# Three kernels in one: the first weight piece's low part moved to GpSimd, the second chunk's gates moved ahead, fewer filler products, later casts

## The chip, the cores and the metric

The kernel runs on one core of a Trainium2 chip. The metric is the device time of one execution in microseconds, the median of several runs. A core has five engines with a queue each: TensorE (matrix products and transposes, PE in the profile), VectorE (DVE), ScalarE (ACT), GpSimd (POOL) and SyncE (SP, which here issues nearly all loads). They run side by side and wait for each other through semaphores; inside one queue the order is that of the program.

## The reference

An mLSTM layer over 2 batches, 8 heads, 768 steps and 40 features, then two mixtures of 8 experts over the 1536 tokens (320 wide, 1024 hidden). The first mixture runs every expert on every token and weighs them by a normalised matrix; the second sends each token to one expert.

```python
# mLSTM, per step t
m_new = np.maximum(f_gate[:, :, t] + m, i_gate[:, :, t])
f_stab = np.exp(f_gate[:, :, t] + m - m_new)
i_stab = np.exp(i_gate[:, :, t] - m_new)
C = f_stab * C + i_stab * einsum('bhd,bhe->bhde', vt, kt)
n = f_stab * n + i_stab * kt
y = sigmoid(o_gate) * (C @ qt) / np.maximum(np.abs(n . qt), 1.0)
...
# first mixture
logits = x @ w_gate
...
for e in range(E):
    out += P[:, e:e + 1] * (np.maximum(x @ w1[e], 0.0) @ w2[e])
# second mixture: the same product, only for the expert with the largest logit
```

## The kernel before

The sequence is cut into 12 tiles of 128 tokens (6 chunks of each batch, the batches alternating). `attn(i)` is a generator for tile `i`: each `yield` is a step, and the program decides by hand when to take the next one. In order, its steps are: the transposes of queries and keys (`turn`), the matrix of decay weights `W` (a product of `R` and the gates, then Relu, Exp, and on GpSimd a masking, `affine_select`, L250, a small copy `wl`, L255, and the scaled keys `ku`, L256), the score products (L268), the next tile's loads, the score product on VectorE (L274), the numerator products on TensorE (L282, in two halves), the numerators and denominators on VectorE (L292 to L308), the state product (L314), the transposes of the result (`transpose_x`, which writes `xh`, the rounded copy, and `xl`, the remainder), and the new state `cbd`. Tiles 0 and 1 are `lead` tiles: they run before anything else, interleaved by hand with `steps(...)`.

`gates(c)` prepares chunk `c` of the gates in eight steps on VectorE, two of which have work on GpSimd too: a scan, two differences, a second scan (L160), a rounding copy (L162) and remainders. `make_R(i)` builds the matrix for tile `i` on VectorE.

The first mixture computes each product of float32 numbers as several products of a rounded part and a remainder. A weight piece comes in by `load_chunk`; `split_chunk` casts it on ScalarE into its high part (L482) and subtracts on VectorE for its low part (L488), then issues the next load. The first expert has three pieces of `w1` (0 to 2) and three of `w2`. `s1_unit` computes one feature tile of 128 of the hidden layer: eight products over three blocks of the inner dimension, then Relu on ScalarE (`hh`, L730) and the remainder on VectorE (`hl`, L731). The first item has two tiles of tokens (0 and 1) and eight feature tiles. In the middle of each feature tile (`mid`) and behind it the program calls a background step `bg_early(u)`, with `u` counting them; the tables `RT`, `AT`, `GT`, `DT` and `OT` say at which `u` a matrix, an attention tile, a chunk of gates, its decays or an output gate's sigmoid starts, and each active generator takes one step per call.

`keep_warm(n, cols)` issues products of a constant whose result nobody reads. The order of the whole start is written out by hand:

```python
        steps(f0, g1, g1)
        steps(f1)
        emit_const1()
        steps(f0, f0)
        keep_warm(4, 256)
        steps(f1, f1)
        low = split_chunk(wait=True)
```

Of the kernel before, what the change touches and what calls it, by code (L numbers as in the profile page):

```python
# [12 lines left out]
ALU = mybir.AluOpType  # L13
# [5 lines left out]
def mlstm_moe_moe_kernel(ctx, tc, q, k, v, i_gate, f_gate, o_gate, wg1, w1a, w2a, wg2, w1b, w2b, out):  # L19
    nc = tc.nc  # L20
    pe, act, dve, pool, sp = nc.tensor, nc.scalar, nc.vector, nc.gpsimd, nc.sync
# [179 lines left out]
    def make_R(i):  # L201
# [12 lines left out]
                              in1=mask[:, b * H + hs.start:b * H + hs.stop].unsqueeze(2).to_broadcast([128, H // n, L]), op=ALU.mult)  # L214
        Rs[i] = R

    def attn(i, ps=pst, lead=False):

        b, c = TILES[i]
# [19 lines left out]
        for g in range(2):  # L239
            pw = ps()  # L240
            pe.matmul(pw, gl_[:, c * L:(c + 1) * L], R[:, 4 * g:4 * g + 4, :].rearrange("k h t -> k (h t)"), start=True, stop=True)
            Wg = W[:, 4 * g:4 * g + 4, :].rearrange("s h t -> s (h t)")
            if i == 0 and g == 0:
                keep_warm(1, 256)
            if lead and g == 1:
                dve.tensor_scalar(out=Wg, in0=pw, scalar1=-1.0, scalar2=0.0, op0=ALU.mult, op1=ALU.max)
            else:
                act.activation(out=Wg, in_=pw, func=AF.Relu, scale=-1.0)
            act.activation(out=Wg, in_=Wg, func=AF.Exp, scale=-1.0)
            pool.affine_select(out=W[:, 4 * g:4 * g + 4, :], in_=W[:, 4 * g:4 * g + 4, :], pattern=[[0, 4], [1, L]],  # L250
                               compare_op=ALU.is_ge, fill=0.0, base=0, channel_multiplier=-1)
        if c < NCH - 1:
            u = ku[i % 2]
            wl = atp.tile([128, H, 1], F32, tag="wl", name="wl")
            pool.tensor_copy(wl, W[:, :, L - 1:L])  # L255
            pool.tensor_tensor(out=u[:, :, 0:D], in0=ks[j][:, :, 0:D], in1=wl.to_broadcast([128, H, D]), op=ALU.mult)  # L256
        yield
        if not lead:
            turn(qs[j], qT)
# [6 lines left out]
        for p in range(4):  # L266
            for a in range(2):
                pe.matmul(sc[a][:, p * L:(p + 1) * L], kT[64 * a:64 * a + D, p, :], qT[64 * a:64 * a + D, p, :], start=True, stop=True)  # L268
        yield
        load_tile(i + NB, "qk")  # L270
        yield
        for a in range(2):
# [440 lines left out]
    def s1_unit(t0, nt, ft, mid, cold=False):  # L713
        n = nt * L
        cols = slice(t0 % 4 * L, t0 % 4 * L + n)
        xh_, xl_ = xh[t0 // 4], xl[t0 // 4]
        fs = slice(ft * 128, (ft + 1) * 128)
        p = ps1()[:, 0:n]
        pe.matmul(p, w1h[:, 0, fs], xh_[:, 0, cols], start=True, stop=False)  # L719
        pe.matmul(p, w1h[:, 0, fs], xl_[:, 0, cols], start=False, stop=False)  # L720
        pe.matmul(p, w1l[:, 0, fs], xh_[:, 0, cols], start=False, stop=False)  # L721
        pe.matmul(p, w1h[:, 1, fs], xh_[:, 1, cols], start=False, stop=False)  # L722
        mid()
        pe.matmul(p, w1h[:, 1, fs], xl_[:, 1, cols], start=False, stop=False)  # L724
        pe.matmul(p, w1l[:, 1, fs], xh_[:, 1, cols], start=False, stop=False)
        if cold:
            keep_warm(3, 256)
        pe.matmul(p, w1h[:, 2, fs], xh_[:, 2, cols], start=False, stop=False)
        pe.matmul(p, w1l[:, 2, fs], xh_[:, 2, cols], start=False, stop=True)  # L729
        act.activation(out=hh[:, ft, 0:n], in_=p, func=AF.Relu)  # L730
        dve.scalar_tensor_tensor(out=hl[:, ft, 0:n], in0=p, scalar=0.0, in1=f32(hh[:, ft, 0:n]), op0=ALU.max, op1=ALU.subtract)  # L731
# [18 lines left out]
    def moe1(bg):  # L750
# [44 lines left out]
        for n, (t0, nt, e) in enumerate(ITEMS):  # L795
            newe = n > 0 and (ITEMS[n - 1][2] != e)
            nxt = n + 1 < len(ITEMS) and ITEMS[n + 1][2] != e
            sv, nsv = seven(n), seven(n + 1)
            s2 = pieces(n)
            total = len(s2)  # L800
            sums = make_sums() if nxt and nsv else None
            if sv:
                wide = t0[1] is not None
                todo = left_over
                left_over = []
                nf = 2 if wide else 3

                def step(j, k):
                    if newe and ((j, k) in ((0, 0), (0, 1), (1, 2)) if wide else j < 3 and k == 2):
                        split_chunk(hi=None if wide else pool)  # L810
                    if sums is not None and (wide or j < 3 and k == 2):
                        for _ in range(2 if wide else 3):
                            next(sums, None)
                s1_seven(t0, lambda x: todo[x](), lambda x: s2[x]() if x < nf else None, step)
                s2 = s2[nf:]
                first = nf
            else:
                assert not left_over
                for ft in range(NF):
                    s1_unit(t0, nt, ft, lambda: bg(n, 2 * ft), n == 0 and ft == 0)  # L820
                    if newe and (ft < 3 if n < EARLY - 2 else ft in (0, 2, 4)) or n == 0 and ft in (2, 4, 6):
                        split_chunk()
                    if sums is not None and ft > 3:
                        next(sums, None)
                        next(sums, None)
                    bg(n, 2 * ft + 1)
                first = 0
            if n == CLASSIC - 1:
                close_x()
                open_late()  # L830
            work = make_w() if nxt and nsv else None
            x2 = make_x(1) if n == SEVEN else None
            for x, f in enumerate(s2):
                u = first + x
                if nsv and u >= total - 2:
                    left_over.append(f)
                else:
                    f()
                if n == SEVEN:
                    for _ in range(2):  # L840
                        next(x2, None)
                if work is not None:
                    next(work, None)
                elif nxt and not nsv and u in ((3, 5, 7) if sv else (1, 3, 5)):
                    split_chunk()
                if not sv:
                    bg(n, 2 * NF + u)
            if work is not None:
                drain(work)
# [584 lines left out]
    with tc.manual_schedule():  # L1434
# [27 lines left out]
        def steps(*fs):  # L1462
            for f in fs:
                next(f)
# [4 lines left out]
        steps(f0, f1)  # L1469
        steps(f0, g1, g1)  # L1470
        steps(f1)
        emit_const1()
        steps(f0, f0)
        keep_warm(4, 256)
        steps(f1, f1)
        low = split_chunk(wait=True)
        for t in range(2):
            act.activation(out=so[t], in_=so[t], func=AF.Sigmoid)
        act.preload_act_table(AF.Exp)
        keep_warm(3)  # L1480
        steps(f0, f0, f0)
        steps(f1)
        steps(f0)
        low()
        keep_warm(2)
        steps(f1, f1, f1)
        steps(f0)
        steps(f1)
# [7 lines left out]
        load_tile(3, "o")  # L1496
        active = [g1, g1]

        RT = {3: 2, 6: 3, 17: 4, 27: 5, 37: 6, 47: 7, 55: 8, 63: 9, 71: 10, 79: 11}
        AT = {5: 2, 8: 3, 20: 4, 30: 5, 40: 6, 50: 7, 58: 8, 66: 9, 74: 10, 82: 11}  # L1500
        GT = {6: 2, 26: 3, 43: 4, 59: 5}
        DT = {5: 1, 20: 2, 36: 3, 54: 4, 70: 5}
# [142 lines left out]
```

## Time and profile before

| | |
|---|---|
| median of 3 runs | 948.32 us (948.24 to 949.23) |
| the profiled execution | 948.92 us |
| its span, first to last instruction | 947.1 us |
| mean granted TensorE clock | 0.997 of full speed |
| TensorE busy | 924.8 us, 98% of the span |
| VectorE, ScalarE, GpSimd busy | 625.7, 457.9, 249.3 us |

The times of the rows are microseconds from the start of the span. Busy time of TensorE is modelled at the end of each product, so a busy TensorE is not one at its peak; the spans of GpSimd's instructions are rough. The chain of waits follows the work that ended last back through what released each step: what stands on it sets the end, what does not is hidden.

### The profile page before, as it was taken

Reading aid. Unit: us, or ns where it says so; the run is one execution under the profiler, and the core shown is the slowest. Engines: PE = TensorE matmul, PEld = TensorE weight load, DVE = VectorE, ACT = ScalarE, POOL = GpSimd, SP = SyncE. Lnnn points to the kernel's source line nnn. Section 1 sums busy time; section 2 is a strip of 40 time slices with the busy share of each in tenths; the row PEclk is TensorE's granted clock in tenths of the full one; section 3 lists DMA queues with packets and bytes.
Section 4 is the critical chain, followed back from the end, with each engine's and each line's share of the span. In section 5 each row is a group of like instructions: output and inputs, shape, how many; then the busy total and the mean of one; then the engine's idle time right before and its main releaser. Section 6 shows DMA issues by size and latency. Waiting matters only on the chain.

```text
span 947.1 us, 15365 instructions
## 1 busy us (share of the span) xinstructions
PE 924.8 (98%) x5729; PEld 832.3 (88%) x5729; DVE 625.7 (66%) x1324; ACT 457.9 (48%) x802; POOL 249.3 (26%) x267
## 2 busy tenths in 40 slices
PE   8999999999999999999999999999999999899995
PEld 6888888988999998999998889999889988678995
DVE  8767766667766877475755748485535468965772
ACT  5666546343445565252535535253432144565662
POOL 4323321001006341406041141502231012324411
PEclk9999999999999999999999999999999999999998
DMA  9825431333334103021210302122090034687540
GB/s 198 193 42 113 101 85 34 90 87 102 88 93 133 58 1 117 17 78 56 78 57 3 115 17 81 53 78 66 22 368 30 15 99 117 211 244 224 154 116 20
DMA packets 93711, 91.28 MB, mean 96 GB/s; under 512 B 54845, under 2 KB 82495, under 8 KB 93632
## 3 DMA queue, kind: packets, MB, share of 16 engines
q1 hardware_dynamic: 91424, 83.50, 31.5%
q0 software_dynamic: 2208, 6.75, 2.2%
q8 instruction: 47, 0.77, 0.3%
q14 instruction: 32, 0.26, 0.1%
HBM read 86.29 MB, written 4.76 MB: 96 GB/s over the span
## 4 chain that ended last, share of the span: by engine, by line
PE 89%; DVE 5%; ACT 2%; issue 2%; DMA 1%; POOL 1%; SPq 0%; DVEq 0%; POOLq 0%; ACTq 0%
PE a L619 17%; PE s L735 8%; PE s L736 8%; PE s L737 8%; PE s L1293 4%; PE a L735 3%; PE a L737 3%; PE a L736 3%; PE s L619 3%; PE a L282 2%; PE s L719 2%; PE s L724 2%; PE s L1226 2%; PE s L729 2%; PE s L721 2%; PE s L722 2%
## 5 line engine op out<-in xcount | busy, mean ns | idle before, releaser
L735 PE MATMUL s<-w2h,hh 128*128 128x320 f32 x544 | 171.4, 315 | 0.0
L737 PE MATMUL s<-w2h,hl 128*128 128x320 f32 x544 | 168.2, 309 | 0.0
L736 PE MATMUL s<-w2l,hh 128*128 128x320 f32 x544 | 168.1, 309 | 0.0
L488 POOL TENSOR_TENSOR w2l<-raw,w2h 128x960 fp32r<-128x960 f32 (+1 forms) x24 | 50.0, 2096 | 228.8 <-ACT w2h L482 228.5
L735 PEld LDWEIGHTS s<-w2h,hh 128*128 128x128 f32 x544 | 102.3, 188 | 2.0
L736 PEld LDWEIGHTS s<-w2l,hh 128*128 128x128 f32 x544 | 102.4, 188 | 1.6
L737 PEld LDWEIGHTS s<-w2h,hl 128*128 128x128 f32 x544 | 102.1, 188 | 0.1
L730 ACT ACTIVATE hh<-s 128x512 fp32r<-128x512 f32 (+1 forms) x88 | 49.1, 558 | 95.9 <-PE s L729 95.8
L731 DVE SCALAR_TENSOR_TENSOR hl<-s,hh 128x512 fp32r<-128x512 f32 (+1 forms) x88 | 56.3, 640 | 57.5 <-ACT hh L730 56.0
L619 PE MATMUL a<-th,w 128*128 128x512 f32 (+1 forms) x224 | 80.5, 366 | 0.0
L619 PE MATMUL a<-ts,wx 96*128 96x512 f32 (+1 forms) x192 | 70.7, 368 | 0.5 <-DVE wx L601 0.5
L735 PE MATMUL a<-w2h,hh 128*128 128x320 f32 x224 | 69.3, 309 | 0.0
L737 PE MATMUL a<-w2h,hl 128*128 128x320 f32 x224 | 69.2, 309 | 0.0
L736 PE MATMUL a<-w2l,hh 128*128 128x320 f32 x224 | 69.1, 309 | 0.0
L763 DVE SCALAR_TENSOR_TENSOR acc<-s,probs,acc 128x320 f32<-128x320 f32 x68 | 37.3, 548 | 39.3 <-PE s L737 38.9
L654 ACT COPY pu<-a 128x512 f32<-128x512 f32 (+1 forms) x32 | 17.1, 533 | 88.3 <-PE a L619 82.9
L646 DVE SCALAR_TENSOR_TENSOR hl<-s,hh 128x512 fp32r<-128x512 f32 (+1 forms) x64 | 39.6, 619 | 30.0 <-ACT hh L642 30.0
L642 ACT ACTIVATE hh<-a 128x512 fp32r<-128x512 f32 (+1 forms) x64 | 34.9, 546 | 36.9 <-DVE a L649 34.4
L646 DVE SCALAR_TENSOR_TENSOR hl<-a,hh 128x512 fp32r<-128x512 f32 (+1 forms) x64 | 39.9, 623 | 15.1 <-ACT hh L642 12.4
L619 PEld LDWEIGHTS a<-th,w 128*128 128x128 f32 x224 | 42.3, 189 | 5.8
L619 PE MATMUL a<-tl,w 128*128 128x512 f32 (+1 forms) x128 | 46.9, 366 | 0.0
L736 PEld LDWEIGHTS a<-w2l,hh 128*128 128x128 f32 x224 | 42.1, 188 | 1.5
(389 smaller groups left out, 2430.0 us busy)
## 6 DMA issues: line engine op xcount, KB each, us to landing
raw<-in_moe_w_dram SPq DMA_DIRECT2D x30, 512.0 KB
raw<-in_moe_w_dram SPq DMA_DIRECT2D x30, 480.0 KB
raw<-in_moe_w_dram SPq DMA_DIRECT2D x39, 320.0 KB
raw<-in_moe_w_dram SPq DMA_DIRECT2D x40, 256.0 KB
wr<-in_moe_w_dram SPq DMA_DIRECT2D x8, 1024.0 KB
w2raw<-in_moe_w_dram SPq DMA_DIRECT2D x12, 640.0 KB
raw<-in_moe_w_dram SPq DMA_DIRECT2D x42, 128.0 KB
q<-in_q_dram SPq DMA_DIRECT2D x12, 160.0 KB
```

The lines of the kernel that those rows point to most:

```text
L282: pe.matmul(pn[:, h * V:(h + 1) * V], W[:, h, :], vs[j][:, h, :], start=True, stop=True)
L488: eng.tensor_tensor(out=l, in0=rv, in1=f32(h), op=ALU.subtract)
L619: pe.matmul(bank, w, x, start=(first and n == 0), stop=(n == 3), skip_group_check=True)
L642: act.activation(out=hh[:, f, c], in_=p, func=AF.Relu)
L646: dve.scalar_tensor_tensor(out=hl[:, f, c], in0=p, scalar=0.0, in1=f32(hh[:, f, c]), op0=ALU.max, op1=ALU.subtract)
L730: act.activation(out=hh[:, ft, 0:n], in_=p, func=AF.Relu)
L731: dve.scalar_tensor_tensor(out=hl[:, ft, 0:n], in0=p, scalar=0.0, in1=f32(hh[:, ft, 0:n]), op0=ALU.max, op1=ALU.subtract)
L735: pe.matmul(p[:, 0:DM], hh[:, f, c], w2h[:, w[n], :], start=(first and n == 0), stop=False)
L736: pe.matmul(p[:, 0:DM], hh[:, f, c], w2l[:, w[n], :], start=False, stop=False)
L737: pe.matmul(p[:, 0:DM], hl[:, f, c], w2h[:, w[n], :], start=False, stop=(last and n == len(cuts) - 1))
L763: dve.scalar_tensor_tensor(out=acc[:, tt, 0:DM], in0=p[:, 0:DM], scalar=probs[:, tt, e:e + 1], in1=acc[:, tt, 0:DM], op0=ALU.mult, op1=ALU ...
L1293: pe.matmul(p, a[:, k, fs], b[:, k, xs], start=(k == 0 and n == 0), stop=(k == 2 and n == 1))
```

## The change

Five edits, all in the first 45 us of the program:

- The low part of the first weight piece is taken by GpSimd instead of VectorE. It is issued inside tile 1's attention, ahead of tile 1's scaled keys, which wait behind it on GpSimd.
- Four of the gate steps of chunk 1 are taken between tile 1's score products and its score product on VectorE; before, the background did them during the first feature tiles. The constants of `emit_const1` follow. The matrix of tile 2 is built at background step 2 instead of 3.
- The fillers in the start are fewer: `keep_warm(3)` becomes `keep_warm(2, 256)` and `keep_warm(2)` becomes `keep_warm(1, 256)`.
- In the first feature tile the products that need only the rounded tokens come first, those with the remainders later.
- The three pieces of the first `w2` are split behind feature tiles 2, 5 and 7 instead of 2, 4 and 6.

```diff
@@ attn(i)
+        def make_ku():
+            pool.tensor_tensor(out=ku[i % 2][:, :, 0:D], in0=ks[j][:, :, 0:D], in1=wl.to_broadcast([128, H, D]), op=ALU.mult)
         if c < NCH - 1:
-            u = ku[i % 2]
             wl = atp.tile([128, H, 1], F32, tag="wl", name="wl")
             pool.tensor_copy(wl, W[:, :, L - 1:L])
-            pool.tensor_tensor(out=u[:, :, 0:D], in0=ks[j][:, :, 0:D], in1=wl.to_broadcast([128, H, D]), op=ALU.mult)
+            if i != 1:
+                make_ku()
...
         yield
+        if i == 1:
+            low0[0]()
+            make_ku()
         load_tile(i + NB, "qk")
@@ s1_unit
-        pe.matmul(p, w1h[:, 0, fs], xh_[:, 0, cols], start=True, stop=False)
-        pe.matmul(p, w1h[:, 0, fs], xl_[:, 0, cols], start=False, stop=False)
-        pe.matmul(p, w1l[:, 0, fs], xh_[:, 0, cols], start=False, stop=False)
-        pe.matmul(p, w1h[:, 1, fs], xh_[:, 1, cols], start=False, stop=False)
-        mid()
-        pe.matmul(p, w1h[:, 1, fs], xl_[:, 1, cols], start=False, stop=False)
-        pe.matmul(p, w1l[:, 1, fs], xh_[:, 1, cols], start=False, stop=False)
+        six = [(w1h, xh_, 0), (w1h, xl_, 0), (w1l, xh_, 0), (w1h, xh_, 1), (w1h, xl_, 1), (w1l, xh_, 1)]
+        if cold:
+            six = [six[z] for z in (0, 2, 3, 5, 1, 4)]
+        for z, (w, x, k) in enumerate(six):
+            if z == 4:
+                mid()
+            pe.matmul(p, w[:, k, fs], x[:, k, cols], start=(z == 0), stop=False)
@@ moe1
-                    if newe and (ft < 3 if n < EARLY - 2 else ft in (0, 2, 4)) or n == 0 and ft in (2, 4, 6):
+                    if newe and (ft < 3 if n < EARLY - 2 else ft in (0, 2, 4)) or n == 0 and ft in (2, 5, 7):
                         split_chunk()
@@ the start
         steps(f1)
-        emit_const1()
         steps(f0, f0)
         keep_warm(4, 256)
-        steps(f1, f1)
-        low = split_chunk(wait=True)
+        steps(f1)
+        low0.append(split_chunk(pool, wait=True))
+        steps(f1, g1, g1, g1, g1)
+        emit_const1()
         for t in range(2):
             act.activation(out=so[t], in_=so[t], func=AF.Sigmoid)
         act.preload_act_table(AF.Exp)
-        keep_warm(3)
+        keep_warm(2, 256)
         steps(f0, f0, f0)
         steps(f1)
         steps(f0)
-        low()
-        keep_warm(2)
+        keep_warm(1, 256)
         steps(f1, f1, f1)
...
-        RT = {3: 2, 6: 3, 17: 4, 27: 5, 37: 6, 47: 7, 55: 8, 63: 9, 71: 10, 79: 11}
+        RT = {2: 2, 6: 3, 17: 4, 27: 5, 37: 6, 47: 7, 55: 8, 63: 9, 71: 10, 79: 11}
```

## Rows read from the trace of the kernel before

**Rows 1.** The page, part 1: busy time, share of the span, instructions.
```profile
PE 924.8 (98%) x5729; PEld 832.3 (88%) x5729; DVE 625.7 (66%) x1324; ACT 457.9 (48%) x802; POOL 249.3 (26%) x267
```
**Rows 2.** Windows: stretch, length, busy by engine, granted clock, DMA share, GB/s.
```profile
20.00:24.00 4.00, 3.05 (x19) 2.11 (x20) 3.86 (x8) 0.98 (x3) 0.00 (x0) 1.00 1.13 254
...
30.00:40.00 10.00, 8.95 (x80) 7.76 (x80) 6.33 (x14) 9.31 (x20) 5.76 (x11) 1.00 0.82 167
40.00:50.00 10.00, 10.00 (x84) 10.00 (x84) 7.88 (x19) 2.34 (x5) 0.92 (x2) 1.00 0.65 131
```
**Rows 3.** Chain of waits, 17 to 40 us: start, length, engine, tile, line.
```profile
17.19 1.14 DVE w L488
...
22.42 1.24 DVE w L488
...
25.06 0.39 ACT hh L730
...
33.95 0.88 ACT w2h L482
...
35.05 0.67 PE a L227 x4
...
39.15 0.82 PE a L282 x8
```
**Rows 4.** Timeline of VectorE, 14 to 25 us: start, length, line, operation, [idle before].
```profile
14.06 1.29 DVE L274 TENSOR_TENSOR W<-s,W 128x512 f32<-128x512 f32 x2 [1.00 <-POOL wl L255]
15.58 0.17 DVE L292 COPY num<-a 128x8 f32<-128x8 f32 x1 [0.22 <-PE a L282]
...
16.06 0.17 DVE L301 SCALAR_TENSOR_TENSOR den<-num 128x8 f32<-128x8 f32 x1
...
17.11 1.22 DVE L488 TENSOR_TENSOR w<-raw,w 128x1024 fp32r<-128x1024 f32 x1
...
23.56 0.27 DVE L158 TENSOR_TENSOR acc<-acc 16x128 f32<-16x128 f32 x1
23.87 0.41 DVE L160 TENSOR_TENSOR_SCAN acc<-msk,acc 16x128 f32<-16x128 f32 x1
...
24.88 0.20 DVE L162 CAST gx<-acc 16x128 fp32r<-16x128 f32 x1
```
**Rows 5.** Timeline of GpSimd, 12 to 15 us.
```profile
12.56 1.21 POOL L250 TENSOR_SCALAR_AFFINE_SELECT W<-W 128x512 f32<-128x512 f32 x2
13.84 0.19 POOL L255 COPY wl<-W 128x8 f32<-128x8 f32 x1
14.12 0.72 POOL L256 TENSOR_TENSOR ku<-k,wl 128x320 f32<-128x320 f32 x1
```
**Rows 6.** Line 488 on GpSimd, 675 to 690 us: ns min/median/max, first and last start.
```profile
L488 POOL TENSOR_TENSOR w<-raw,w x3: 2413/2415/2421, 681.0 to 685.8; 128x1024 fp32r<-128x1024 f32 x3
```
**Rows 7.** Timelines of VectorE and GpSimd, 68 to 71 and 862 to 866 us.
```profile
69.78 0.84 DVE L160 TENSOR_TENSOR_SCAN acc<-msk,acc 16x128 f32<-16x128 f32 x1
...
68.54 1.81 POOL L250 TENSOR_SCALAR_AFFINE_SELECT W<-W 128x512 f32<-128x512 f32 x2 [3.29 <-ACT W L249]
...
864.38 1.17 DVE L1250 TENSOR_TENSOR oid<-acc,big 128x1 int32<-128x1 f32 x1
...
862.47 3.06 POOL L1199 TENSOR_TENSOR w2l<-w2raw,w2h 128x640 fp32r<-128x640 f32 x2
```
**Rows 8.** Timelines of VectorE, ScalarE and GpSimd, 27 to 38 us.
```profile
27.86 1.16 DVE L488 TENSOR_TENSOR w2l<-raw,w2h 128x960 fp32r<-128x960 f32 x1 [0.15 <-ACT w2h L482]
...
34.87 1.59 DVE L488 TENSOR_TENSOR w2l<-raw,w2h 128x960 fp32r<-128x960 f32 x1 [0.46 <-DMA wgr<-in_moe_w_gate_dram]
...
37.34 1.27 DVE L274 TENSOR_TENSOR W<-a,W 128x512 f32<-128x512 f32 x2
...
36.22 0.39 ACT L730 ACTIVATE hh<-s 128x256 fp32r<-128x256 f32 x1
...
34.72 0.72 POOL L256 TENSOR_TENSOR ku<-k,wl 128x320 f32<-128x320 f32 x1
```

More of the change, by code (lines that the diff above doesn't have):

```diff
@@ L215, in make_R @@
         Rs[i] = R
+    low0 = []
     def attn(i, ps=pst, lead=False):
```

## The prediction

> **What bounds the kernel now.** I read the page first. TensorE is busy 98% of the span [rows 1], so a change elsewhere can pay only where TensorE waits. Next the stretches of the start: 20 to 24 us holds 3.05 us of TensorE work in 4.00, 30 to 40 us holds 8.95 in 10, from 40 us on there is no gap, and the granted clock is 1.00 in all of them [rows 2]. So the change acts on about 0.95 + 1 us of idle time, plus products that merely fill waits. Third, the chain of waits says whose work fills the gaps [rows 3]. From 15.58 to 23.66 us it is almost wholly VectorE's: the numerators of tile 0, the low part of the first weight piece (17.19), those of tile 1, the second low part, four small splits, the third low part (22.42). TensorE's last product of the first feature tile waits for that third one. From 25.06 to 35.05 us the chain is ScalarE's; the last part of it is the cast of the second output-weight piece (33.95, 0.88 us). With the key transposes at 35.05 it passes to TensorE. Two things can therefore move the end: the time at which VectorE finishes the third low part, and the time at which ScalarE lets those transposes go.
>
> **The low part on GpSimd.** VectorE spends 1.22 us on it, 1.14 of them on the chain [rows 3, 4]. The same shape costs GpSimd 2.41 us [rows 6]. It follows the small copy at 13.84 and would run from about 14.1 to 16.5. VectorE now ends it at 18.33 (17.19 + 1.14) and nobody waits for it then, so it is hidden; a delay beyond 18.3 would use up what cover there is. Before it leaves GpSimd, four things queue: the scaled key tile of tile 1 (0.72 us, [rows 5]), two gate steps, and the memsets of the constants. The scaled key tile then ends near 17.6 us; TensorE reads it behind the transposes of tile 0, which wait for tile 0's numerators (17.19 now), so it is hardly late. The load issued behind the low part goes into SP's queue three issues earlier, ahead of tile 4's queries and keys, which nothing reads before tiles 2 and 3 are through: nothing. VectorE's 0.22 us wait before the numerators (15.35 to 15.58, for TensorE) goes as well, since two filler products of 256 columns replace three of 512. Gross gain: 1.14 + 0.22 = 1.36 us.
>
> **The gates in the idle stretch.** VectorE stands still for 1.00 us before the score product at 14.06 [rows 4]. Three gate steps go there; undisturbed they need 0.31 + 0.44 + 0.24 = 0.99 us (starts at 23.56 and 23.87, then 0.41 and 0.20 with the usual step). They would just fit and cost nothing. But GpSimd is masking tile 1's weights at that time, 12.56 to 13.77 [rows 5], and the two engines do disturb each other. The same scan, started at 69.78 during two such maskings, took 0.84 us against 0.41, and the maskings 1.81 against 1.21 [rows 4, 5, 7]. At 864.38 a one-element instruction of VectorE took 1.17 us: it ended when the second of GpSimd's two subtractions did (862.47 + 3.06 = 865.53) [rows 7]. An instruction with both inputs in SBUF waits out GpSimd's whole instruction. The score product, with one input from PSUM, does not: 1.29 us for two, with GpSimd's multiplication beside it [rows 4, 5]. So I price the three steps at the idle 1.00 us plus 0.4 us, the scan's measured excess; bounds 0 and a whole GpSimd instruction (a rival below).
>
> The Trainium skill says this as a rule ("SBUF — State Buffer", section "Who interferes with whom"): VectorE's second SBUF input comes through a read port shared with GpSimd, the one that issues second blocks until the other has finished, and issue order alone decides. The trace agrees with it at 864.38. Taken at its word it gives either nothing or a full 2.4 us for each meeting, instead of the 0.4 and 0.5 us that I use.
>
> **The same conflict in the numerators.** With the score product 0.4 us late (14.45 to 15.74), the numerators of tile 0 start at 15.74. Two instructions read PSUM; the denominator, 0.48 us later as now (15.58 to 16.06 [rows 4]), so near 16.25, has both inputs in SBUF and meets the low part, which then runs from about 14.45 to 16.85. Price 0.5 us (bounds 0 and 0.6). The normalising product meets the scaled key tile: 0.2 us (0 and 0.5, from the 0.72 us of [rows 5]). Tile 1's chain meets the two gate steps: 0.1 us (0 to 0.3).
>
> Sum for VectorE's chain: 1.36 − 0.4 − 0.5 − 0.2 − 0.1 = **0.16 us** earlier, between −0.4 and +1.36.
>
> **Edits priced at nothing.** The new order of the first tile's products lets four of them run before tile 1's low parts are there, but the last still waits for the third low part (22.42 + 1.24), so the end of that tile does not move. If that cover went (the third low part ready before the products), the order would be worth part of the 0.95 us that TensorE is idle in that stretch [rows 2]. The three gate steps that leave the stretch after 23.56 and the weight matrix of tile 2 built one step earlier free VectorE and TensorE inside a stretch that ScalarE sets from 25.06 to 35.05 [rows 3]: nothing. Tile 2's matrix now stands ahead of the second feature tile's low part on VectorE and delays it; the bank that this low part frees is wanted only behind tile 2's matrix products on TensorE, and these wait for the same matrix. If ScalarE were not the bound there, these edits would be worth up to the 0.92 us that the three instructions' steps take. Of the fillers taken away only those ahead of tile 0's numerator products stood before waiting work, and they are counted above (the 0.22 us); the others shorten TensorE's queue where it waits for VectorE anyway.
>
> **The casts one feature tile later.** Now the second cast sits between the fifth feature tile's activation and the small decay activations that free the bank for tile 3's key transposes. Without it these start 0.88 us sooner, at 34.17 instead of 35.05, and everything behind them on TensorE follows: tile 2's numerator products, now at 39.15, could start at 38.27. But they need the score product, and VectorE's queue now has the second low part ahead of it. That one waits for the cast, which follows the sixth activation (ends 36.61 now [rows 8], 35.73 then): cast to 36.61, low part 1.16 us (27.86; the 1.59 at 34.87 met GpSimd's multiplication at 34.72, which will be over), first half of the score product 0.64 (half of 1.27) gives 38.45 with the steps between. So VectorE, not TensorE, is last there, and the gain is 39.15 − 38.45 = 0.7 us; less 0.1 for the new wait's own signal I take **0.6 us**. Bounds: 0.1, if the low part is again stretched by 0.43 to 0.44, and 0.88. The third cast falls behind the eighth activation; its piece is wanted by the last part of the output stage, well behind the numerator products at 39.15.
>
> **The sum.** 0.16 + 0.6 = 0.76 us. The profiled execution took 948.92 us (span 947.1, and 1.8 us around it), so it would become 948.16. It lies 0.60 above the median of the runs, 948.32, and taken from that the forecast is **947.6 us**, 0.08% less. Behind 40 us TensorE has no gap for 10 us [rows 2], so what it gains there should last.
>
> **Rivals.** *VectorE keeps the whole gain* (chance 0.19): the meetings happen in other gaps and cost nothing. For it: the starts differ by a few tenths, GpSimd's spans are rough, and each price above supposes that two instructions meet. Against it: three meetings would all have to miss. Then 1.36 + 0.6 to 0.88, about 946.3. *The gates lose the port* (0.12): the place is 14.2 us. The scan or the cast after it must ask before GpSimd's low part does. My reckoning has the cast ask near 14.2 and the low part near 14.4 (13.84 + 0.28 + the scan's delay). If that margin of 0.25 us is used up, VectorE stands until about 16.5, the score product starts near 17.2. From its start to the end of the third low part it is 9.60 us now (14.06 to 23.66), 8.24 without the gross gain: it ends near 25.4, 1.8 us lost, 0.6 regained by the cast: 949.5. By the Trainium skill's rule on issue order this is what happens on that side of the margin. *The cast gives nothing* (0.14): the second low part is stretched again or TensorE meets another wait before 41 us. Then 0.16 + 0.1: 948.1. *The clock falls* (0.05): fewer fillers stand between 13 and 22 us. Against it: it stayed at 2.4 GHz (1.00) with only 3.05 us busy in the 4 us from 20 on [rows 2]. At 1.2 GHz these 3.05 us would take 6.1, 2.1 beyond the stretch: 949.7.
>
> The Trainium skill ("TensorE: Matmul & The Clock Gate", section "What's actually happening") says that the clock is halved by default and that activity releases it, which speaks against removing fillers. Here the rows show no fall, and the change leaves some in each of the three places.
>
> **Numbers.** The forecast has a chance of 0.50, with its own range 947.0 to 948.2. What a measurement of this kernel can tell from no change is about 0.2%, 1.9 us: below 946.4 or above 950.2. Only the better part of the first rival and its unknowns reach below (0.15), and only the tails of the second and fourth above (0.06); 0.79 lies within. The range 946.3 to 949.7 leaves out about 0.06 below and 0.09 above.
>
> **What would show it.** Right: VectorE's three gate steps between 13.0 and 14.5 with the scan at 0.6 us or more; the first denominator at 0.4 us or more instead of 0.17; the third low part ending 23.2 to 23.8; the key transposes of tile 3 near 34.0 and the numerator products near 38.3. Wrong: the scan or the cast behind it at 2 us or more (the port is lost); the denominators at 0.17 us and the third low part near 22.3 (full gain); granted clock under 1.00 before 36 us; the numerator products still near 39.

## The result and the profile after

The change makes the kernel slower: 954.16 us (952.83 to 955.21, five runs) against 948.32; the ratio is 1.0061, with a 95% interval of 1.005 to 1.0072. The forecast was 947.6, in a range that ended at 949.7. The profiled execution took 954.16 us, with a span of 952.4 and a mean granted clock of 0.99 (0.997 before). TensorE's own work has hardly changed in number, but its busy time has grown by 5 us beside that of [rows 1]:

```profile
PE 929.8 (98%) x5727; PEld 837.6 (88%) x5727; DVE 627.1 (66%) x1323; ACT 458.7 (48%) x802; POOL 251.0 (26%) x268
```

Nearly as many products that take longer point to a lower clock, which the windows below show. To see where the trouble begins, read VectorE's timeline (start, length, line, operation; line numbers are those of the changed kernel, where L281 is the score product, L308 and L309 the denominators and L495 the low part on VectorE or GpSimd):

```profile
12.63 0.93 DVE L158 TENSOR_TENSOR acc<-acc 16x128 f32<-16x128 f32 x1
13.60 0.41 DVE L160 TENSOR_TENSOR_SCAN acc<-msk,acc 16x128 f32<-16x128 f32 x1
14.05 2.19 DVE L162 CAST gx<-acc 16x128 fp32r<-16x128 f32 x1
16.17 1.27 DVE L281 TENSOR_TENSOR W<-s,W 128x512 f32<-128x512 f32 x2
...
17.84 0.15 DVE L308 SCALAR_TENSOR_TENSOR den<-num 128x8 f32<-128x8 f32 x1
18.02 0.43 DVE L309 TENSOR_SCALAR den<-den 128x8 f32<-128x8 f32 x1
...
24.71 0.42 DVE L359 TENSOR_TENSOR xl<-s,xh 128x256 fp32r<-128x256 f32 x1 [1.55 <-ACT xh L358]
...
25.48 1.23 DVE L495 TENSOR_TENSOR w<-raw,w 128x1024 fp32r<-128x1024 f32 x1
```

and GpSimd's:

```profile
13.49 0.19 POOL L258 COPY wl<-W 128x8 f32<-128x8 f32 x1
13.65 2.52 POOL L495 TENSOR_TENSOR w<-raw,w 128x1024 fp32r<-128x1024 f32 x1
16.12 0.72 POOL L255 TENSOR_TENSOR ku<-k,wl 128x320 f32<-128x320 f32 x1
```

The rounding copy of 16 x 128 elements, 0.20 us in [rows 4], takes 2.19 us: GpSimd's low part began 0.40 us ahead of it, and the copy ends (16.24) just after the low part does (16.17). The three gate steps that were to fill 1.00 us of idle time last from 12.63 to 16.24. Tile 1's score product follows them at 16.17 (the records of neighbours overlap by some hundredths).

TensorE, which needs that product, stands still. The waits of TensorE (12 to 50 us: total, times, longest):

```profile
PE s L289 <- DVE W L281: 2.0, 1, 2.0
PE a L243 <- DVE R L213: 0.7, 1, 0.7
```

In the kernel before, the same question gives these two first:

```profile
PE a L227 <- ACT dec L189: 0.8, 1, 0.8
PE a L241 <- DVE R L213: 0.7, 1, 0.7
```

The windows of the kernel after (stretch, length, busy time of TensorE, weight loads, VectorE, ScalarE, GpSimd, then the granted clock):

```profile
14.00:15.00 1.00, 0.87 (x8) 0.66 (x7) 0.96 (x2) 0.99 (x3) 1.00 (x1) 1.00 0.94 245
15.00:16.00 1.00, 0.00 (x0) 0.00 (x0) 1.00 (x1) 0.98 (x2) 1.00 (x1) 1.00 1.31 195
16.00:17.00 1.00, 0.10 (x1) 0.11 (x1) 1.00 (x3) 0.99 (x2) 1.00 (x3) 1.00 1.11 174
17.00:18.00 1.00, 1.00 (x10) 1.00 (x10) 0.99 (x4) 0.60 (x1) 0.88 (x4) 1.00 0.95 158
18.00:19.00 1.00, 1.00 (x7) 1.00 (x7) 0.91 (x3) 0.00 (x0) 0.96 (x5) 0.57 0.41 67
...
24.00:25.00 1.00, 1.00 (x4) 0.36 (x3) 0.29 (x1) 0.53 (x2) 0.00 (x0) 0.52 1.14 324
...
32.00:33.00 1.00, 0.25 (x3) 0.11 (x1) 1.00 (x4) 0.97 (x3) 0.86 (x1) 1.00 0.99 136
...
35.00:36.00 1.00, 1.00 (x12) 1.00 (x13) 0.13 (x1) 1.00 (x2) 1.00 (x2) 0.60 0.25 21
...
41.00:42.00 1.00, 1.00 (x14) 1.00 (x12) 0.55 (x2) 0.98 (x2) 0.00 (x0) 0.50 0.00 0
```

Between 15 and 17 us TensorE does next to nothing; within the next two its clock drops to 1.2 GHz: 0.57 over 18 to 19 us is a fall at 18.1, and by 0.52 over 24 to 25 it is back only at 25.0. Behind a second gap, the wait for the matrix near 32 us, the same happens from 35.2 to 42.0. A gap does not always bring a fall: in the kernel before, TensorE has that wait too, and one of 0.8 us, and its clock is 1.00 from 10 to 50 us. The chain of waits shows what comes of it; GpSimd's low part now stands on it:

```profile
13.65 2.52 POOL w L495
...
19.77 5.39 DMA raw<-in_moe_w_dram
...
25.48 1.24 DVE w L495
...
46.15 0.22 PE s L742
```

Between the two low parts this chain goes by GpSimd's scaled keys and memsets and by a load, not by the copy and the score product; the profile infers its links, so the cause is read from the timelines above and not from it. By them the third low part (25.48) stands in VectorE's queue behind the remainder of tile 1 (L359), for which VectorE was idle 1.55 us: that one waited for ScalarE's rounded copy, and this for TensorE's transposes, which take 0.63 us at half clock instead of 0.44. The last line is the first product of the output stage. In the kernel before the same step of its chain is

```profile
41.34 0.22 PE s L735
```

so 4.81 us of the loss are there at 46 us. To make traces comparable, the table below cuts this stretch at three events: **A** from the end of tile 0's score product to the start of tile 1's (before: 13.06 to 14.06, the idle 1.00 of [rows 4]), **B** on to the end of the third low part, **C** on to the output stage. Tile 0's ended at 12.71 after the change (12.04 + 0.67).

| profiled execution | A | B | C | sum | against before |
|---|---|---|---|---|---|
| before | 1.00 | 9.60 | 17.68 | 28.28 | |
| after | 3.46 | 10.55 | 19.43 | 33.44 | +5.16 |

### The profile page after: what moved, and what is told of

It is laid out like the page before. It is cut to its first block, busy times and chain, and to the rows that moved or that the text cites. A ratio compares the mean times of both kernels' runs of the same rounds, so it can differ in the third digit from the quotient of the medians.

```text
span 952.4 us, 15364 instructions
## 1 busy us (share of the span) xinstructions
PE 929.8 (98%) x5727; PEld 837.6 (88%) x5727; DVE 627.1 (66%) x1323; ACT 458.7 (48%) x802; POOL 251.0 (26%) x268
## 4 chain that ended last, share of the span: by engine, by line
PE 88%; DVE 5%; issue 2%; POOL 2%; DMA 1%; ACT 1%; SPq 0%; DVEq 0%; POOLq 0%; ACTq 0%
PE a L626 17%; PE s L732 10%; PE s L742 8%; PE s L744 8%; PE s L743 8%; PE s L1300 4%; PE a L742 3%; PE a L744 3%; PE a L743 3%; PE s L626 3%; PE a L289 2%; PE s L1233 2%; PE s L736 2%; PE s L735 2%; PE s L1282 1%
## 5 line engine op out<-in xcount | busy, mean ns | idle before, releaser
L732 PE MATMUL s<-xh,w 128*128 128x512 f32 (+1 forms) x352 | 118.5, 381 | 0.9 <-DVE hl L738 0.7
L495 POOL TENSOR_TENSOR w2l<-raw,w2h 128x960 fp32r<-128x960 f32 (+1 forms) x24 | 50.1, 2097 | 228.8 <-ACT w2h L489 228.5
L732 PEld LDWEIGHTS s<-xh,w 128*128 128x128 f32 x352 | 65.5, 190 | 15.3 <-DVE hl L738 3.1
L732 PE MATMUL s<-xl,w 128*128 128x512 f32 (+1 forms) x176 | 67.4, 384 | 0.0
```

Of the source, the lines that this page charges most:

```text
L495: eng.tensor_tensor(out=l, in0=rv, in1=f32(h), op=ALU.subtract)
L732: pe.matmul(p, w[:, k, fs], x[:, k, cols], start=(z == 0), stop=False)
```

## The experiments

"A fall" below is a run whose mean granted clock is 0.995 or less. One stretch of 7 us at half speed, as in the windows above, takes 3.5/952 = 0.004 off the mean; undisturbed runs lie at 0.996 to 0.998. A fall half as long takes 0.002 and can hide from this measure: two of the profiled executions below have a mean of 0.996 and a fall of 3.4 us, so the counts are lower bounds. The kernel before, run again beside each group of experiments, had 3 falls in 95 runs. The changed kernel had one or more in each of its five.

**Only two gate steps ahead of tile 1's score product.** The copy goes back to the background; the low part stays on GpSimd.

```diff
-        steps(f1, g1, g1, g1, g1)
+        steps(f1, g1, g1)
```

> The whole change, but the rounding copy of the gates (L162) goes back to the background; only the two steps up to the scan stay in the idle stretch. Port theory (the copy that waits 2.2 us behind GpSimd's low part makes the score product late, TensorE's 2.0 us wait follows, and its clock falls because of that wait): the score product starts near 14.1 instead of 16.2, granted clock 1.00 from 13 to 30 us, 946.5 to 949. Filler theory (the clock falls because fillers were taken away, the late score product costs only its own 2 us): the score product starts near 14.1 as well, but the clock still falls between 16 and 25 us, 950.5 to 952.5.

Measured: 949.03 us against 947.94 (ratio 1.0013, 1.0003 to 1.0023). VectorE's timeline:

```profile
13.90 1.25 DVE L281 TENSOR_TENSOR W<-s,W 128x512 f32<-128x512 f32 x2
...
15.55 0.61 DVE L308 SCALAR_TENSOR_TENSOR den<-num 128x8 f32<-128x8 f32 x1
16.20 1.66 DVE L309 TENSOR_SCALAR den<-den 128x8 f32<-128x8 f32 x1
...
22.82 1.23 DVE L495 TENSOR_TENSOR w<-raw,w 128x1024 fp32r<-128x1024 f32 x1
```

GpSimd's beside it:

```profile
13.61 2.53 POOL L495 TENSOR_TENSOR w<-raw,w 128x1024 fp32r<-128x1024 f32 x1
16.10 0.72 POOL L255 TENSOR_TENSOR ku<-k,wl 128x320 f32<-128x320 f32 x1
...
17.15 0.68 POOL L131 MEMSET cbd<- 128x328 f32 x2
```

The score product is on time, and most of the loss is gone. But the low part now stops the denominators: the first takes 0.61 us and ends at 16.16, when the low part has ended (16.14); the second takes 1.66 and ends at 17.86, behind the scaled keys and the memsets that follow (17.83). Both take 0.17 in the kernel before. The 1.14 us moved off VectorE come back as 0.44 + 1.49 us of waiting. Nine of ten runs had a fall. The profiled one (949.32 us, mean clock 0.996) had a shorter one, well behind the start of the output stage, as its windows show:

```profile
65.00:66.00 1.00, 1.00 (x8) 1.00 (x8) 0.97 (x3) 0.36 (x1) 0.21 (x1) 0.68 0.00 0
66.00:67.00 1.00, 1.00 (x7) 1.00 (x6) 0.00 (x0) 0.00 (x0) 0.00 (x0) 0.50 0.00 0
...
68.00:69.00 1.00, 1.00 (x5) 0.81 (x5) 0.93 (x3) 0.54 (x1) 0.00 (x0) 0.62 0.00 0
```

That is a fall from 65.4 to 68.8 us, after 12 us in which TensorE's windows show no idle time. None of the ten runs is known to be free of a fall, so their price in this kernel can't be read from its times.

**The whole change with the fillers of before.**

```diff
-        keep_warm(2, 256)
+        keep_warm(3)
...
-        keep_warm(1, 256)
+        keep_warm(2)
```

> The whole change with the fillers of before (three and two of 512 columns). Both theories: the copy still takes about 2.2 us and the score product starts near 16.2; TensorE's wait before tile 1's numerator products shrinks from 2.0 to about 1.3 us. Filler theory: clock 1.00 throughout, 949 to 950. Port theory: the wait is still there, and the clock falls unless 1.3 us are too short for it: 952 to 954, or 949.5 with the clock at 1.00, which would leave both open.

Measured: 950.49 us (ratio 1.0033, 1.0021 to 1.0045); a fall in all seven runs. The copy still takes 2.20 us, the score product starts at 16.15, and TensorE still waits 1.3 us. The loss is 2.55 us instead of 5.84, so the fillers are worth 3.3 us of it. They don't prevent the falls, but the mean clocks are 0.990 to 0.995 instead of 0.988 to 0.991. The median lies in neither theory's range: the wait for the score product and the fillers both count.

**Tile 1's scaled keys ahead of the low part on GpSimd.**

```diff
-            low0[0]()
             make_ku()
+            low0[0]()
```

> The whole change, but on GpSimd tile 1's scaled keys (0.7 us) go ahead of the low part (2.5 us), so the copy meets the short instruction. Port theory: the copy takes 0.4 to 0.8 us instead of 2.2, the score product starts near 14.6, clock 1.00 to 30 us, 947 to 949. Filler theory: the clock falls all the same, 950.5 to 952.5. A third idea (any meeting costs 2 us): the score product stays near 16.

Measured: 952.21 us (ratio 1.0051, 1.0034 to 1.0068), a fall in all four runs. VectorE's timeline and the windows:

```profile
14.02 0.56 DVE L162 CAST gx<-acc 16x128 fp32r<-16x128 f32 x1
14.51 1.27 DVE L281 TENSOR_TENSOR W<-s,W 128x512 f32<-128x512 f32 x2
```

```profile
14.00:15.00 1.00, 0.84 (x8) 0.63 (x7) 0.98 (x2) 0.99 (x3) 1.00 (x2) 1.00 0.95 232
15.00:16.00 1.00, 0.76 (x6) 0.77 (x6) 1.00 (x4) 0.98 (x2) 1.00 (x1) 0.87 1.27 185
16.00:17.00 1.00, 1.00 (x7) 1.00 (x6) 0.97 (x3) 0.99 (x2) 1.00 (x2) 0.50 0.99 177
```

The copy got past the scaled keys with 0.56 us, and TensorE waited only 0.4 us, yet its clock fell (at 15.7) just as it does behind a wait of 2.0. It fell once more from 66.9 to 70.4 us. A long wait for the score product, then, is not needed for a fall.

**Only the fewer fillers**, in the kernel before (the two lines above, reversed).

> The kernel before with only the fewer fillers of the change. Port theory: TensorE waits for VectorE anyway, clock 1.00, 948.0 to 948.5. Filler theory: the clock falls between 16 and 25 us, 951 to 953.

Measured: 948.07 us, ratio 1.0005 (0.9995 to 1.0015), but the runs split: six without a fall took 947.08 to 948.21, four with one 948.25 to 951.04. Fewer fillers alone let the clock fall in four runs of ten; the score product was on time (13.86). Where the clock held, fewer fillers were a small gain: in the profiled execution, one of the six, B is 9.30 instead of 9.60.

**Only the later casts**, in the kernel before.

```diff
-... or n == 0 and ft in (2, 4, 6):
+... or n == 0 and ft in (2, 5, 7):
```

> The kernel before with one part of the change, the casts behind feature tiles 2, 5 and 7. The prediction's own term: the key transposes of tile 3 near 34.2 instead of 35.05, the numerator products near 38.5 instead of 39.15, the output stage 0.6 us earlier, the median 947.3. The rival that the cast gives nothing: the output stage where it is (41.3) and the median within 0.2 us of the kernel before. A third way, taken from the changed kernel's second fall of the clock: the moved work leaves TensorE a gap near 32 to 35 us, the clock falls to half there in some runs, and these are 2 us or more slower.

Measured: 946.85 us against 947.66, ratio 0.999 (0.9981 to 0.9999), no fall in eleven runs. TensorE's timeline:

```profile
33.77 0.66 PE L227 MATMUL a<-ident,k 128*128 128x128 f32 x4
...
38.06 1.08 PE L282 MATMUL a<-v,W 128*128 128x41 f32 x8 [0.18 <-DVE W L274]
```

The key transposes stand at 33.77; that trace runs 0.38 us ahead of the one before already at the third low part (22.04 against 22.42), so they gained 35.05 − 33.77 − 0.38 = 0.90 us, and the numerator products, now behind VectorE's score product, 38.99 (39.15 in the chain) − 38.06 − 0.38 = 0.55.

**Two gate steps and the fillers of before** (the first two edits together).

> The changed kernel with only two gate steps ahead of tile 1's score product (as in the first experiment) and the kernel before's number and size of fillers. If it is the sparser fillers that let the clock fall once the score product is on time: granted clock 0.996 or more in nearly all runs and a median of 947.5 to 948.2, against 949.0 of the first experiment. If the fall has another cause (the work that GpSimd's low part holds up on VectorE, or the gap near 32 us): still about 949 with mean clocks of 0.992 to 0.994.

Measured: 948.3 us against 947.66, ratio 1.0009 (1.0 to 1.0018), one fall in eleven runs. With the clock up, the low part on GpSimd is still no gain: the two denominators take 0.49 and 1.79 us.

**The low part back on VectorE at its old place**, fillers of before, the rest of the change kept (four gate steps in the idle stretch).

```diff
-            low0[0]()
...
-        low0.append(split_chunk(pool, wait=True))
+        low = split_chunk(wait=True)
```

> The changed kernel with the low part back on VectorE at its old place and the fillers of the kernel before; the four gate steps stay in VectorE's idle stretch, the new order of products, the later casts and the matrix one step earlier stay too. If GpSimd's low part is what blocks the gate steps: the rounding copy takes 0.2 to 0.6 us, the score product starts by 14.5, the clock stays at 1.00 and the median is 947 to 948. If four gate steps do not fit into the stretch whatever GpSimd does: the copy or the score product is still 1 us or more late, and the median is 949 or more.

Measured: 948.27 us against 947.66, ratio 1.0004 (0.9995 to 1.0013), four falls in eleven runs. The copy takes 0.56 us and the score product starts 1.82 us behind tile 0's instead of 3.46. Without GpSimd's low part the gate steps cost 0.82 us in A; a shorter B (9.30) and the casts give it back. The seven runs without a fall have a median of 947.53 us.

**The low part on VectorE, but ahead of tile 1's score product**, in the kernel before with the later casts.

```diff
-        low = split_chunk(wait=True)
+        split_chunk()
...
-        low()
```

> The kernel before with the later casts and with the first low part on VectorE still, but ahead of tile 1's score product, where VectorE is idle for 1.00 us, instead of behind tile 0's numerators. If VectorE's chain up to the third low part sets the end: the score product moves to about 14.9 (the low part meets GpSimd's masking and is 0.3 us or more late), the 1.22 us disappear from the chain behind the numerators, the third low part ends about 0.3 to 0.5 us earlier, and the median is 0.5 to 1.1 us below the kernel before (946.8 to 947.5). If the low part is blocked by the maskings as the gates' copy was by the low part: the score product near 16 and the median 949 or more, with the clock fallen.

Measured: 946.39 us against 947.66, ratio 0.9987 (0.9978 to 0.9996), two falls in eleven runs. VectorE's timeline, and GpSimd's small copy of the weights' last column:

```profile
13.62 1.36 DVE L488 TENSOR_TENSOR w<-raw,w 128x1024 fp32r<-128x1024 f32 x1 [0.44 <-ACT w L482]
15.06 1.29 DVE L274 TENSOR_TENSOR W<-s,W 128x512 f32<-128x512 f32 x2
...
22.02 1.23 DVE L488 TENSOR_TENSOR w<-raw,w 128x1024 fp32r<-128x1024 f32 x1
```

```profile
13.96 1.07 POOL L255 COPY wl<-W 128x8 f32<-128x8 f32 x1
```

Here VectorE came first, and GpSimd waits: its copy takes 1.07 us instead of the 0.19 of [rows 5]. The score product is 0.88 us later than before, and B falls to 8.20, so the low part costs 0.88 us in A instead of 1.39 in B. This is the best version found. Its profiled execution took 948.01 us, 1.6 above the median, at a mean clock of 0.996: it has one of the short falls, from 64.7 to 68.1 us, behind the stretches of the table.

**The same with the new order of the first feature tile's products.**

```diff
+        if cold:
+            six = [six[z] for z in (0, 2, 3, 5, 1, 4)]
```

> The kernel of the experiment with VectorE's early low part and later casts, with one part of the change more: the first feature tile's products that need only the rounded tokens come first. The prediction priced this order at nothing, because the last product still waits for the third low part: then within 0.2 us of that kernel (946.2 to 946.6), and the third wait for the remainder of tile 1 moves from the second product to a later one. If the order is worth part of the 0.8 us that TensorE waits there: 945.6 to 946.1.

Measured: 947.96 us against 948.71, ratio 0.9994 (0.9985 to 1.0003), four falls in eleven runs. B and C are those of the version before it (8.20 and 17.24), so the order is worth nothing there. No gain shows in the times either: the median gains 0.75 us instead of 1.27, and the runs without a fall 1.0 instead of 1.4. Whether it makes falls likelier (four against two) these numbers can't say.

**The whole change with nine fillers in the first place**, so that TensorE is busy while it waits for the score product.

```diff
-        keep_warm(2, 256)
+        keep_warm(9)
...
-        keep_warm(1, 256)
+        keep_warm(2)
```

> The whole change, but with nine fillers of 512 columns in the first place (two of 256 in the changed kernel) and two of 512 in the second, so that TensorE has no gap while it waits for tile 1's score product. The gate steps still lose the port. If the clock is what turned the late score product into 5.8 us: the rounding copy still takes about 2 us and the score product still starts near 16, but the granted clock is 0.996 or more and the median is 947.8 to 949.5 (a score product 2.1 us late, less 1.36 gained behind it, less the casts' 0.6, gives about 948.1 to 948.5). If the late score product alone is the price: 952 or more, fillers or not. If both falls of the clock have causes of their own: the first goes, the one from 35 us on stays, and the median is 950 to 952.

Measured: 951.14 us against 948.71, ratio 1.0028 (1.0018 to 1.0038), five falls in nine runs; the four without one took 949.81, 949.83, 949.83 and 951.75. The first expectation's range (to 949.5) ends just below three of these four, and the median lies in the third's. The profiled execution is one of the four. VectorE's timeline and one step of the chain:

```profile
14.63 2.20 DVE L162 CAST gx<-acc 16x128 fp32r<-16x128 f32 x1
16.76 1.27 DVE L281 TENSOR_TENSOR W<-s,W 128x512 f32<-128x512 f32 x2
...
23.90 1.23 DVE L495 TENSOR_TENSOR w<-raw,w 128x1024 fp32r<-128x1024 f32 x1
```

```profile
42.40 0.22 PE s L742
```

The port is lost as before, and A is the 3.46 us of the changed kernel. B is 8.38 instead of 10.55 and C 17.26 instead of 19.43: with the clock up, 2.17 us are gained in each.

**Nine fillers, and three more in the second gap** near 31 us.

```diff
+            if u == 8:
+                keep_warm(3)
```

> The experiment with nine fillers, and three fillers of 512 columns more in TensorE's second gap, the 0.7 us in which it waits for the matrix of tile 3 near 31 us. If the falls of the clock that were left in five of nine runs of that kernel begin behind this gap: 0.996 in nearly all runs and a median of 949.8 to 950.3, about 1.1 us above the kernel before, which is then the price of the lost port alone. If they begin elsewhere (in the sparse stretch of 22 to 26 us): still half of the runs at 0.993 to 0.995, and a median of 950.5 to 952.

Measured: 948.92 us against 947.43, ratio 1.0018 (1.0009 to 1.0028), one fall in eleven runs. With the second gap filled the falls nearly go, which fits falls that begin behind it; no trace of a fallen run of nine fillers is kept that would show the place. With the clock held, what remains of the loss is 1.5 us: the price of the lost port, less what the other edits gain.

**Scaled keys first, and the fillers of before.**

> The whole change, but tile 1's scaled keys ahead of the low part on GpSimd, and the fillers of the kernel before. If the two causes add (the port lost at the copy, and fillers too sparse for TensorE's clock), both are gone here: the copy takes about 0.6 us, the score product starts near 14.5, the denominators of tile 0 lose 1 to 2 us to the low part, the clock stays at 0.996 or more, and the median is 947.8 to 948.8, no better than the kernel before. If sparse fillers do not matter beside a score product 0.4 us late: clocks near 0.99 and 951 to 953 as without the fillers.

Measured: 948.8 us against 948.71, ratio 1.0005 (0.9996 to 1.0014), two falls in eleven runs, where the same kernel with the sparse fillers had one in each of four. The copy takes 0.57 us and the denominators 0.68 and 0.38 us.

The stretches of these executions, each the profiled one:

| | A | B | C | sum | against before |
|---|---|---|---|---|---|
| two gate steps (no fall in A to C) | 1.23 | 10.16 | 17.24 | 28.63 | +0.35 |
| two gate steps, fillers of before | 1.22 | 10.28 | 17.22 | 28.72 | +0.44 |
| keys first (clock fallen in B) | 1.83 | 11.01 | 17.26 | 30.10 | +1.82 |
| keys first, fillers of before | 1.82 | 8.95 | 17.25 | 28.02 | −0.26 |
| nine fillers | 3.46 | 8.38 | 17.26 | 29.10 | +0.82 |
| nine fillers and three | 3.47 | 8.37 | 17.25 | 29.09 | +0.81 |
| low part on VectorE, old place | 1.82 | 9.30 | 17.21 | 28.33 | +0.05 |
| casts only | 1.01 | 9.59 | 17.23 | 27.83 | −0.45 |
| casts, low part on VectorE early | 1.88 | 8.20 | 17.22 | 27.30 | −0.98 |

## Why the prediction was wrong

The step that failed is the pricing of **the gates in the idle stretch**: three steps "at the idle 1.00 us plus 0.4 us", and behind it the margin of the second rival, by which the copy would ask for the port near 14.2 and the low part near 14.4. They asked at 14.05 and 13.65, in a trace that runs 0.35 us ahead of the one before (tile 0's score product ends at 12.71 instead of 13.06): at 14.40 and 14.00 by the prediction's times, the copy 0.2 us later than reckoned and the low part 0.4 earlier. Both terms of that margin were wrong. On GpSimd the low part started 0.16 us behind the start of the small copy `wl` (13.49 to 13.65), where I had taken 0.28, and the maskings, which I had delayed by the scan, took their usual 1.22 us. On VectorE the first gate step, which the prediction took at its undisturbed step of 0.31 us, lasted 0.93: it met the maskings, and its end (13.56) lies behind theirs (13.43). The scan, whose excess was the 0.4 us, took 0.41 as if alone. So A, the place of the three steps, is 3.46 us, 2.06 more than the 1.40 forecast.

With that the rival named **the gates lose the port** (chance 0.12) is what happened, and its own sum was near: it gave 949.5, 1.2 us above the median before, where the runs with the clock held are 1.1 us (three of the four of nine fillers, around 949.83 against 948.71) and 1.5 us above (948.92 against 947.43). Its terms were less near: it had the score product at 17.2, and by the same times it started at 16.52 (16.17 + 0.35), since the copy ends with the low part. The Trainium skill ("SBUF — State Buffer", section "Who interferes with whom") says that a copy or a one-input arithmetic instruction can, if its operands allow it, enter a mode that takes the shared pair too, and that the second to issue blocks until the first is done. The traces agree with the blocking, in both directions: 2.19 us for the copy, 1.07 us for GpSimd's copy behind VectorE's low part. The prediction had quoted the rule and then priced the meeting at 0.4 us, by a scan that had met a masking.

The rest, 4.34 of the 5.16 us of the table, is **the clock**, which had a chance of 0.05. The size of one fall came out right (2.1 forecast, 2.17 measured in B and in C), by luck: the forecast slowed the 3.05 us of work of a 4 us stretch, and the measured falls last 6.8 us each, which would be 3.4 us for a TensorE that never waits. That there would be two, and that they would come together with the lost port, was not seen. The argument against it was that 20 to 24 us, at 3.05 busy in 4.00 us [rows 2], showed no fall. That a stretch so sparse shows no fall does not mean that one sparser will not: the fewer fillers alone brought a fall in four runs of ten. So "edits priced at nothing" was wrong about the fillers as well: beyond the 0.22 us counted for them, which did come (B is 9.30 with fewer fillers alone), they were holding the clock in part of the runs. The Trainium skill's page on TensorE, "TensorE: Matmul & The Clock Gate", section "What's actually happening", describes a clock that is halved unless activity releases it; the traces agree, with 0.50 behind both gaps of the changed kernel.

Term by term, by the table:

- *Gross gain on VectorE's chain*, 1.36 us forecast: 9.60 − 8.38 = 1.22 with the clock held. Right, but only where the low part meets the copy instead of the denominators.
- *The same conflict in the numerators*, 0.5 + 0.2 + 0.1 us: in the changed kernel nearly absent (0.15 and 0.43 for the two denominators), since the low part was over by then. Where it did meet them, with two gate steps, it was 0.44 us on the instruction named, within its bounds, and 1.49 us on the one behind it, which the prediction did not count. Where the steps were late by less, with the scaled keys first and the fillers of before, the first denominator lost 0.51 us, the price forecast, and the second, which was not counted, 0.21; that version comes nearest to what the prediction assumed, and A was 1.82 there instead of 1.40. In no order tried do the gate steps and the low part on GpSimd together beat the kernel before: A and B are 11.39 us (two gate steps), 11.84 (nine fillers) and 10.77 (keys first, fillers of before) against 10.60. With the scaled keys first the low part by itself does pay a little: the same with the low part on VectorE has 11.12.
- *The casts*, 0.6 us: 0.45 in the table and 0.81 in the medians, with the transposes 0.90 and the numerator products 0.55 earlier. Right in mechanism and size. The changed kernel has this gain too.
- *Edits priced at nothing*: the order of products, nothing, as said; the matrix one step earlier and the constants behind the gates were not tried alone. The constants' memsets, moved behind the low part, are by the times (17.86 behind 17.83) what the second denominator waits for in the experiment with two gate steps.

With these sizes the prediction's own sum is 2.46 − 1.22 − 0.42 = +0.82 us without a fall, and two falls of 2.17 us make 5.16. The two profiled executions differ by 5.24 (954.16 − 948.92); the medians by 5.84, since the one of before lay 0.60 above its median.

Two things stay open. Why the clock falls in some runs of a kernel and not in others, the traces don't show. Each gap filled made it rarer, yet the kernel before has waits of 0.7 and 0.8 us without a fall, and four of the traces (two gate steps; fillers of before; keys first; low part early on VectorE) have a short one between 64 and 73 us, where no wait stands in the 12 us before it. And what the falls of the kernel with two gate steps cost can't be told, since none of its runs is known to have none.

## What to carry to other kernels

Before moving work to an engine that shares a port with a busy one, write down the start of every instruction on both around it, with every earlier one at its disturbed length; if the order is decided by a quarter of a microsecond, price the case in which it comes out the other way. An idle stretch of VectorE is best filled with an instruction that can stand first (here the low part itself, 946.39 us) instead of making a second engine compete for it. Products that nobody reads may be holding TensorE's clock: take them away only after checking over many runs, since a median of ten can hide a fall in four, and a mean clock of 0.996 a short one.

## What the runs showed of the hardware

- A 16 x 128 rounding copy on VectorE, 0.20 us alone, took 2.19 us beside a 2.5 us subtraction of GpSimd and 0.56 us beside a 0.77 us multiplication. An instruction on 128 x 8 elements, 0.17 us alone, took 1.66 us, through several short GpSimd instructions in a row, memsets among them.
- VectorE does the same to GpSimd: a copy of 128 x 8 took 1.07 us instead of 0.19 beside a subtraction of 1.36 us that had started 0.34 us earlier.
- TensorE's clock went from 2.4 to 1.2 GHz for 6.8 us behind a wait of 0.4 us (keys first, from 15.7 us) as well as behind one of 2.0, in the longer case 1.2 us after work had resumed (16.89 to 18.1). Waits of 0.7 and 0.8 us in the kernel before brought no fall.
- Other falls last 3.4 us, as from 65.4 to 68.8 with two gate steps, after 12 us without idle time of TensorE in the windows.
